# Even and odd tokens: v two tokens to a row, q and k as 96 rows, diagonal key blocks shared by two heads

## The chip, the core and the metric

The kernel runs on one core of a Trainium2 chip. The metric is the device time of one execution in microseconds. The engines are PE (TensorE matmuls; its weight loads are listed apart as PEld), ACT (ScalarE), DVE (VectorE), POOL (GpSimd, which here issues nearly all DMAs, and those that cast float32 to bf16 in flight) and SP (which issues most of the output DMAs).[...]

## What is computed

Attention with two kinds of heads over 4 batches, 8 heads, 768 tokens and head size 64, and then a soft mixture of experts over slots (8 experts of 4 slots). A "retrieval" head sees all earlier tokens; a "streaming" head sees the first 4 tokens and the last 64.

```
scores = q @ k.T / 8
keep   = causal                                   # retrieval heads
keep   = causal & (col < 4 | row - col < 64)      # streaming heads
a      = softmax(where(keep, scores, -1e9))
x      = concat over heads of a @ v               # 3072 x 512

logits = x @ phi                                  # 3072 x 32
slots  = softmax over tokens(logits).T @ x        # 32 x 512
y[e]   = relu(slots[e] @ w1[e]) @ w2[e]           # 512 -> 1024 -> 512
out    = softmax over slots(logits) @ y           # 3072 x 512
```

q, k and v are 6.3 MB each in float32, w1 and w2 16.8 MB each, and the output is 6.3 MB. Which heads are retrieval heads is data, read from a tensor, so every causal block is computed for every head, and the masks are made on the chip.

## The kernel before, in words

The unit of work is a pair of heads n of one batch (16 pairs). The two heads lie on partitions 0 to 63 and 64 to 127 of the transposed tiles, so a score matmul (L167, contraction over 64 rows) of one head uses one half of the array's rows. The order is written out by hand (L320 to L392): in step n the scores and exponentials of pair n are interleaved with the product with v of pair n-1.

Loading (L106 to L119). q and k come as 64 partitions for a head, 12 tokens (3 KB in float32) to a row. `load_v` (L116) brings four heads of v in one DMA, one token (256 bytes) to a partition and block: tile `vb` is [128, 4 heads, 6 blocks of 128 tokens, 64 + 2], the last two columns being ones. The weights come through `w_load` (L129), a few to a step: w1 of all experts, then w2 of experts 0 to 4, 12 more DMAs of 1 MB (as bf16) behind w1[0]. w2 of experts 5 to 7 is loaded in halves (L398) into the places of tiles that are done: of the masks (`msk`, free after the last mask) and of the two `pT` tiles (free after the product with v). All of these DMAs go through the one queue of POOL.

Transposing (L135 to L151). For each pair and each of q and k: 24 matmuls of 64x64 against the identity into a PSUM tile of tag `tr` (two buffers), then one copy to SBUF that puts the tokens in order: q by DVE (L148), k by ACT (L151).

Scores and exponentials (L160 to L172). The 21 causal blocks of 128 keys x 128 queries come in six chunks of up to 512 columns a head. Chunk c of both heads takes two PSUM banks (tag `sc`, two buffers), and one ACT instruction exponentiates it into `pT`. Chunks 0 to 2 hold the blocks on and next to the diagonal and are multiplied by 0/1 masks on DVE (L174 to L184). Streaming heads lose farther blocks through `vf` (L157), a copy of v that is zeroed for them by `fmask`.

Product with v (L186 to L194). For query block i and head hh, i+1 matmuls with 65 columns (64 of v and the column of ones, whose sum is the softmax denominator), 42 a pair. `norm` (L196) divides three blocks of both heads at a time.

Step n, on PE in this order: S0, product of blocks 0 to 2 of pair n-1 (and for n mod 4 = 2 the logits of the batch before), S1, transposes of q for pair n+1, S2, block 3, transposes of x of pair n-2, S3, transposes of k for n+1, S4, block 4, S5, block 5 (and for n mod 4 = 3 the dispatch of tokens to slots). ACT copies Tk of n+1 between E4 and E5; DVE takes norm, copy of Tq, masks, copy of x, masks, `vf`, norm. Setup (L253 to L305) builds the identity, the mask values and the masks of the first two heads; those of the others are made in steps 0 to 2, and small tables in step 3 (`setup_late`).

After the last pair (L428 on): last product with v, last logits, slot sums, first layer (w1), second layer (`second`, L508, experts 4 to 7: first the left half of the columns, then the right), and the output rows, left halves of the first 12 of 24 rows a partition first.

Of the kernel before, what the change touches and what calls it, by code (L numbers as in the profile page):

```python
# [19 lines left out]
NPT = 2688  # L20

CHUNKS = [
    (0, 512, [(0, 0, 2), (1, 1, 2)]),
    (512, 512, [(2, 2, 2), (3, 3, 2)]),
    (1024, 384, [(4, 4, 2), (5, 5, 1)]),
    (1408, 512, [(0, 2, 4)]),
    (1920, 512, [(1, 3, 3), (3, 5, 1)]),
    (2432, 256, [(2, 4, 2)]),
]
BLK = {}  # L30
for _o, _l, _parts in CHUNKS:
    for _j, _i0, _n in _parts:
        for _x in range(_n):
            BLK[_j, _i0 + _x] = _o
            _o += 128
# [3 lines left out]
def kernel(  # L39
# [39 lines left out]
    w2s = [single([P, 8, DM], BF16, f"w2_{e}") for e in range(NE - 3)] + [None] * 3  # L79
# [11 lines left out]
    msk = single([P, H, 640], BF16, "msk")  # L91
    fmask = single([P, H, 4, 66], BF16, "fmask")
# [7 lines left out]
    r0 = single([P, H], F32, "r0")  # L100
    thr = single([P, H], F32, "thr")
    vbs = [single([P, 4, 6, 66], BF16, f"vb{i}") for i in range(3)]
# [3 lines left out]
    def load_qk(pairs, order="qk"):  # L106
        b, h, c = pairs[0] // 4, 2 * (pairs[0] % 4), 2 * len(pairs)
        t = raw.tile([P, 2, 2, S], BF16, tag="raw", name="raw")
        for which in order:
            src, d, z = (q, qraw, 0) if which == "q" else (k, kraw, 1)  # L110
            nc.gpsimd.dma_start(t[:, z, :len(pairs)],  # L111
                                src[b, h:h + c].rearrange("(y h) (p s) d -> (h p) y (s d)", h=2, s=12))
            for x, n in enumerate(pairs):
                d[n] = t[:, z, x]

    def load_v(m):  # L116
        b, h = m // 2, 4 * (m % 2)
        nc.gpsimd.dma_start(vbs[m % 3].rearrange("p h j d -> p (h j) d")[:, :, :D],  # L118
                            v[b, h:h + 4].rearrange("h (j p) d -> p (h j) d", p=P))  # L119
# [8 lines left out]
    def w_load(upto):  # L128
        while wi[0] < min(upto, 2 * NE - 3):  # L129
            e = wi[0] % NE  # L130
            dst, src = ((w1s, w1v), (w2s, w2v))[wi[0] // NE]
            nc.gpsimd.dma_start(dst[e], src[e])
            wi[0] += 1

    def transposes(n, which):  # L135
        src = (qraw if which == "q" else kraw)[n]
        tp = trp.tile([P, 12, 64], BF16, tag="tr", name="tp" + which)
        for s in range(12):
            for hh in range(2):
                po = slice(64 * hh, 64 * hh + 64)  # L140
                nc.tensor.transpose(tp[po, s, :], src[po, 64 * s:64 * s + 64], ident[po, po])  # L141
        return tp

    def evac(n, which, tp):
        dst = qkT.tile([P, S], BF16, tag="T" + which, name="T" + which)
        o, i = dst.rearrange("c (p s) -> c p s", s=12), tp.rearrange("c s p -> c p s")
        if which == "q":
            nc.vector.tensor_copy(o, i)  # L148
            qT[n] = dst
        else:  # L150
            nc.scalar.copy(o, i)  # L151
            kT[n] = dst

    def vfar(n):
        h = 2 * (n % 4)
        t = vfp.tile([P, 2, 4, 66], BF16, tag="vf", name="vf")
        nc.vector.tensor_mul(t, vb(n)[:, :, :4, :], fmask[:, h:h + 2])  # L157
        vf[n] = t

    def scores(n, c):  # L160
        o, ln, parts = CHUNKS[c]
        sc = scp.tile([P, 2, 512], F32, tag="sc", name="sc")
        at = 0
        for j, i0, cnt in parts:
            for hh in range(2):
                po = 64 * hh
                nc.tensor.matmul(sc[:, hh, at:at + 128 * cnt], kT[n][po:po + 64, j * 128:(j + 1) * 128],  # L167
                                 qT[n][po:po + 64, i0 * 128:(i0 + cnt) * 128], start=True, stop=True)
            at += 128 * cnt
        if c == 0:  # L170
            pT[n] = ptp.tile([P, 2, NPT], BF16, tag="pT", name="pT")
        nc.scalar.activation(pT[n][:, :, o:o + ln], sc[:, :, :ln], ACT.Exp, scale=scale)  # L172

    def mask(n, c):  # L174
        h = 2 * (n % 4)
        if c == 0:
            x, m = pT[n][:, :, 0:512], msk[:, h:h + 2, 0:512]
        elif c == 1:
            x = pT[n][:, :, 512:1024].rearrange("p h (a c) -> p h a c", a=2)
            m0 = msk[:, h:h + 2, 256:512]  # L180
            m = bass.AP(tensor=m0.tensor, offset=m0.offset, ap=[m0.ap[0], m0.ap[1], [0, 2], [1, 256]])
        else:
            x, m = pT[n][:, :, 1024:1408], msk[:, h:h + 2, 256:640]
        nc.vector.tensor_mul(x, x, m)  # L184

    def pvmm(n, i):  # L186
        if i % 3 == 0:
            pv[n] = pvp.tile([P, 3, 2, 65], F32, tag="pv", name="pv")
        for hh in range(2):
            for j in range(i + 1):  # L190
                vv = vb(n) if i - j <= 1 else vf[n]
                o = BLK[j, i]
                nc.tensor.matmul(pv[n][:, i % 3, hh, :], pT[n][:, hh, o:o + 128], vv[:, hh, j, :D + 1],  # L193
                                 start=(j == 0), stop=(j == i))  # L194

    def norm(n, half):  # L196
        b, h = n // 4, 2 * (n % 4)
        if h == 0 and half == 0:
            xb[b] = xp.tile([P, 6, DM], BF16, tag="xb", name="xb")
        rs = small.tile([P, 3, 2, 1], F32, tag="rs", name="rs")  # L200
        nc.vector.reciprocal(rs, pv[n][:, :, :, 64:65])  # L201
        nc.vector.tensor_mul(  # L202
            xb[b][:, 3 * half:3 * half + 3, h * D:(h + 2) * D].rearrange("p i (h d) -> p i h d", h=2),
            pv[n][:, :, :, :64], rs.to_broadcast([P, 3, 2, 64]))
# [47 lines left out]
    diff = single([P, 256], F32, "diff")  # L252
    nc.gpsimd.iota(diff, pattern=[[1, 256]], base=0, channel_multiplier=-1,  # L253
# [15 lines left out]
    V.tensor_single_scalar(ident, diff[:, :P], 0.0, op=ALU.is_equal)  # L269
    one_row = single([1, P], BF16, "one_row")  # L270
    V.memset(one_row, 1.0)
    sk = single([P, 1], F32, "sk")
    sk2 = single([P, 1], F32, "sk2")
    ge = single([P, 256], BF16, "ge")
    grade = single([P, 640], BF16, "grade")
    V.tensor_single_scalar(rne, ri.rearrange("p (h c) -> p h c", c=2), 0.0, op=ALU.not_equal)
    V.tensor_tensor(rrow1, rne[:, :, 0], rne[:, :, 1], op=ALU.max)
    rb = trp.tile([P, H], F32, tag="tr", name="rb")
    nc.tensor.matmul(rb, one_row, rrow1, start=True, stop=True)
    V.tensor_single_scalar(ge, diff, 0.0, op=ALU.is_ge)  # L280
    V.scalar_tensor_tensor(grade[:, 256:512], diff, float(window), ge, op0=ALU.is_lt, op1=ALU.mult)
    V.tensor_add(grade[:, 256:512], grade[:, 256:512], ge)
    V.tensor_copy(grade[:, 512:640], grade[:, 256:384])
    V.tensor_single_scalar(sk, diff[:, 0:1], float(-n_sink), op=ALU.is_gt)
    V.tensor_scalar(sk2, sk, 2.0, None, op0=ALU.mult)
    V.scalar_tensor_tensor(grade[:, :256], ge, sk2, grade[:, 256:512], op0=ALU.mult, op1=ALU.max)
    V.tensor_copy(r1, rb)
    V.tensor_scalar(thr, r1, -1.0, 2.0, op0=ALU.mult, op1=ALU.add)
    V.tensor_scalar(r0, r1, sk, None, op0=ALU.max)

    def head_mask(h):
        V.tensor_scalar(msk[:, h], grade, thr[:, h:h + 1], None, op0=ALU.is_ge)

    for which in ("k", "q"):
        evac(0, which, transposes(0, which))
    for h in range(2):
        head_mask(h)
    def far_mask(n):
        h = 2 * n
        V.tensor_copy(fmask[:, h:h + 2, 1:], r1[:, h:h + 2].rearrange("p (h a d) -> p h a d", a=1, d=1).to_broadcast([P, 2, 3, 66]))  # L300
        V.tensor_copy(fmask[:, h:h + 2, 0], r0[:, h:h + 2].rearrange("p (h d) -> p h d", d=1).to_broadcast([P, 2, 66]))

    for t in vbs:
        V.memset(t[:, :, :, D:], 1.0)
# [15 lines left out]
    for n in range(NP):  # L320
# [16 lines left out]
        if n >= 1:  # L337
            for i in range(3):
                pvmm(last, i)
# [6 lines left out]
        if n >= 1:  # L346
            norm(last, 0)
# [3 lines left out]
        mask(n, 0)  # L351
# [4 lines left out]
        if n >= 1:  # L356
            pvmm(last, 3)
        if n >= 2:
            x_transpose(n - 2)
        mask(n, 1)  # L360

        scores(n, 3)
        if 0 < n < NP - 1:
            tk = transposes(n + 1, "k")
        mask(n, 2)

        scores(n, 4)
        if 0 < n < NP - 1:
            evac(n + 1, "k", tk)
        if n >= 1:  # L370
            pvmm(last, 4)
# [6 lines left out]
        if n >= 1:  # L378
            pvmm(last, 5)
# [4 lines left out]
        if n == 0:  # L384
            evac(1, "q", transposes(1, "q"))
            evac(1, "k", transposes(1, "k"))
        if n < 3:
            far_mask(n + 1)
            for h in (2 * n + 2, 2 * n + 3):
                head_mask(h)  # L390
# [10 lines left out]
    w2s[5] = single([P, 8, DM], BF16, "w2_5", tag="msk")  # L401
# [12 lines left out]
    def copies(y, t):  # L414
        g, b0 = y % 3, 2 * (y // 3)
        t = bank(t)
        for x in range(2):
            nc.tensor.matmul(t[:, 256 * x:256 * x + 256], sum4[32 * g:32 * g + 32],  # L418
                             expT[32 * g:32 * g + 32, b0 + x], start=True, stop=True)
# [9 lines left out]
    for i in range(3):  # L429
        pvmm(last, i)  # L430
# [3 lines left out]
    for i in range(3, 6):  # L434
        pvmm(last, i)
# [169 lines left out]
```

The softmax here doesn't subtract the row's maximum and nothing guards it: scores larger than these inputs give would overflow.

## Time and profile before

| | |
|---|---|
| median of 3 runs | 157.21 us (156.84 to 157.72) |
| the profiled execution | 157.49 us, its span 155.7 us |
| PE busy | 118.2 us (76%), 2239 matmuls |
| ACT busy | 109.8 us (71%), 148 instructions |
| DVE busy | 106.8 us (69%), 247 instructions |
| POOL busy | 41.1 us (26%), 57 instructions |
| DMA | 32.85 MB written, mean 211 GB/s; HBM read 52.49 MB |
| exponentials L172 | 96, 83.4 us on ACT |
| product with v L193 | 672 matmuls, 27.5 + 25.3 us on PE |
| copies of Tq L148 | 16, 956 ns each on DVE |
| v loads L118 | 8 of 384 KB, 13.0 us from issue to landing, 1451 ns of POOL each |

Busy times of one engine are sums over instructions. A busy PE is no PE at its peak, since matmuls are pipelined: in the timeline the distance between two starts tells more than a duration. The DMA rate counts bytes written; most loads read twice as many (float32 in, bf16 out). "A <- B" in the waits means that A stood idle until B was done, with total, number and longest wait. The chain of work that ended last is followed back from the last instruction; what stands in it set the end, in this one execution.

### The profile page before, as it was taken

How to read it: one execution, taken by the hardware profiler on the slowest of the kernel's cores; microseconds unless marked ns; L12 is line 12 of the kernel's file. 1: busy time of each engine (PE TensorE's matmuls, PEld its weight loads, DVE VectorE, ACT ScalarE, POOL GpSimd, SP SyncE). 2: the span in 40 equal slices, each digit the busy share in tenths (PEclk: the TensorE clock that was granted, in tenths of full speed). 3: DMA queues.
4: the chain of work that ended last, by engine and by line, in shares of the span. 5: the costliest groups of instructions: out<-in, count | busy, mean ns of one | idle time of the engine just before them, and what ended most of it. 6: DMA issues, size and time to landing. Idle time of an engine off the chain costs nothing. (4 is left out here: it accounts for less than half of the span.)

```text
span 155.7 us, 5051 instructions
## 1 busy us (share of the span) xinstructions
PE 118.2 (76%) x2239; PEld 74.6 (48%) x2239; DVE 106.8 (69%) x247; ACT 109.8 (71%) x148; POOL 41.1 (26%) x57
## 2 busy tenths in 40 slices
PE   6756598878697979977979979778987897449500
PEld 2324365555465645755656556555633476214300
DVE  2896269999987869978769979678735414429700
ACT  3286489979799998999898999999451512408700
POOL 7673043720350260170084200000480000700000
PEclk9975559999999999999999999999999999956975
DMA  3999999999999999999999999999999999977995
GB/s 54 155 184 203 172 218 203 196 187 189 212 219 202 188 216 198 186 222 195 186 219 200 185 211 223 213 217 215 210 223 190 199 196 199 240 290 283 404 355 183
DMA packets 40535, 32.85 MB, mean 211 GB/s; under 512 B 26050, under 2 KB 37826, under 8 KB 38594
## 3 DMA queue, kind: packets, MB, share of 16 engines
q0 software_dynamic: 38208, 27.82, 115.1%
q1 hardware_dynamic: 2306, 4.72, 8.1%
q8 instruction: 17, 0.28, 0.7%
q14 instruction: 4, 0.03, 0.1%
HBM read 52.49 MB, written 6.29 MB: 377 GB/s over the span
## 5 line engine op out<-in xcount | busy, mean ns | idle before, releaser
L172 ACT ACTIVATE pT<-sc 128x1024 bf16<-128x1024 f32 (+1 forms) x96 | 83.4, 923 | 9.3 <-PE sc L167 8.8
L167 PE MATMUL sc<-Tq,Tk 64*128 64x256 bf16 (+3 forms) x320 | 36.5, 292 | 13.6 <-ACT Tk L151 10.0
L193 PEld LDWEIGHTS <-pT 128*128 128x128 bf16 x672 | 24.9, 99 | 12.2 <-issue 8.0
L184 DVE TENSOR_TENSOR pT<-pT,msk 128x1024 bf16<-128x1024 bf16 (+1 forms) x48 | 29.3, 639 | 0.2 <-ACT pT L172 0.2
L193 PE MATMUL pv<-vb,pT 128*128 128x65 bf16 x352 | 27.5, 196 | 0.3 <-DVE xb L202 0.3
L193 PE MATMUL pv<-vf,pT 128*128 128x65 bf16 x320 | 25.3, 197 | 0.0
L167 PEld LDWEIGHTS <-Tk 64*128 64x128 bf16 x320 | 11.2, 95 | 22.6 <-ACT Tk L151 13.2
L141 PEld LDWEIGHTS <-raw 64*64 64x64 bf16 x768 | 15.9, 115 | 10.8 <-issue 7.4
L111 POOL DMA_DIRECT2D raw<-in_q_dram x10 | 6.4, 639 | 49.5 <-PE tpk L141 48.3
L148 DVE COPY Tq<-tpq 128x768 bf16<-128x768 bf16 x16 | 15.3, 956 | 4.8 <-PE tpq L141 4.6
L202 DVE TENSOR_TENSOR xb<-pv,rs 128x384 bf16<-128x384 f32 x32 | 17.8, 557 | 1.1
L151 ACT COPY Tk<-tpk 128x768 bf16<-128x768 bf16 x16 | 12.9, 805 | 5.0 <-PE tpk L141 5.0
L201 DVE RECIPROCAL rs<-pv 128x6 f32<-128x6 f32 x32 | 6.2, 193 | 11.9 <-PE pv L193 11.9
L118 POOL DMA_DIRECT2D vb<-in_v_dram x8 | 11.6, 1451 | 1.1 <-issue 0.9
L141 PE MATMUL tpk<-ident,raw 64*64 64x64 bf16 x384 | 9.8, 202 | 2.3 <-DVE Tq L148 1.3
L399 POOL DMA_DIRECT2D w<-in_moe_w_dram x6 | 5.2, 879 | 22.3 <-PE sc L167 20.1
L141 PE MATMUL tpq<-ident,raw 64*64 64x64 bf16 x384 | 9.6, 200 | 1.7 <-DMA raw<-in_q_dram 1.7
L541 PE MATMUL bank<-slot_out,expR 128*128 128x256 bf16 (+1 forms) x36 | 9.2, 368 | 1.9 <-DVE slot_out L556 0.5
L210 PE MATMUL tpx<-ident,xb 128*128 128x128 bf16 x96 | 8.1, 218 | 2.0 <-ACT expT L224 1.1
L211 DVE COPY xT<-tpx 128x768 bf16<-128x768 bf16 (+1 forms) x17 | 9.0, 528 | 0.8 <-PE tpx L210 0.8
L543 ACT ACTIVATE ot<-bank,rrow 128x512 f32<-128x512 f32 x6 | 3.9, 686 | 6.5 <-PE bank L541 6.5
L541 PEld LDWEIGHTS <-expR 128*128 128x128 bf16 x36 | 5.1, 153 | 6.3 <-issue 5.7
(86 smaller groups left out, 117.3 us busy)
## 6 DMA issues: line engine op xcount, KB each, us to landing
w<-in_moe_w_dram POOLq DMA_DIRECT2D x13, 1024.0 KB, 18.3
vb<-in_v_dram POOLq DMA_DIRECT2D x8, 384.0 KB, 13.0
w<-in_moe_w_dram POOLq DMA_DIRECT2D x6, 512.0 KB, 17.8
raw<-in_q_dram POOLq DMA_DIRECT2D x6, 384.0 KB, 10.2
raw<-in_k_dram POOLq DMA_DIRECT2D x6, 384.0 KB, 11.4
out_dram<-ot SPq DMA_DIRECT2D x2, 1024.0 KB, 4.6
out_dram<-oh SPq DMA_DIRECT2D x3, 512.0 KB, 6.3
out_dram<-oh POOLq DMA_DIRECT2D x2, 512.0 KB, 6.8
```

Source lines behind the costliest of these rows:

```text
L118: nc.gpsimd.dma_start(vbs[m % 3].rearrange("p h j d -> p (h j) d")[:, :, :D], v[b, h:h + 4].rearrange("h (j p) d -> p (h j) d", p=P))
L141: nc.tensor.transpose(tp[po, s, :], src[po, 64 * s:64 * s + 64], ident[po, po])
L148: nc.vector.tensor_copy(o, i)
L151: nc.scalar.copy(o, i)
L167: nc.tensor.matmul(sc[:, hh, at:at + 128 * cnt], kT[n][po:po + 64, j * 128:(j + 1) * 128], qT[n][po:po + 64, i0 * 128:(i0 + cnt) * 128], s ...
L172: nc.scalar.activation(pT[n][:, :, o:o + ln], sc[:, :, :ln], ACT.Exp, scale=scale)
L184: nc.vector.tensor_mul(x, x, m)
L193: nc.tensor.matmul(pv[n][:, i % 3, hh, :], pT[n][:, hh, o:o + 128], vv[:, hh, j, :D + 1], start=(j == 0), stop=(j == i))
L202: nc.vector.tensor_mul(xb[b][:, 3 * half:3 * half + 3, h * D:(h + 2) * D].rearrange("p i (h d) -> p i h d", h=2), pv[n][:, :, :, :64], rs. ...
L210: nc.tensor.transpose(tp[:, i * 128:(i + 1) * 128], xb[b][:, i, hp * 128:(hp + 1) * 128], ident)
L211: nc.vector.tensor_copy(xT[:, hp, i0 * 128:i1 * 128], tp[:, i0 * 128:i1 * 128])
L541: nc.tensor.matmul(op, er[r], slot_out[:, cs], start=True, stop=True)
```

## The change

Loads. v comes as two neighbouring tokens to a partition row, 512 bytes, in three blocks of 256 tokens; a v load is six DMAs, since for the second head of a pair the two halves of the partitions are swapped. q and k come as 96 partitions, 8 tokens (2 KB) to a row, the heads side by side.

Transposes. 16 a tensor and pair instead of 24, of 96 rows to 64 x 96. For q the copy to SBUF keeps the order (8 token residues, 6 blocks, 16 rows), so query columns within a block are permuted; score matmuls read them as runs of 16 elements. For k the copy by ACT separates even and odd tokens.

Scores. A key tile is 128 even or 128 odd tokens of a block of 256. For query block i = 2j only the first half of block j is causal; these halves of two heads are put on the two halves of the partitions of chunk 0: 12 matmuls 64 x 64 x 128. The other chunks: 4, 4, 8, 4 and 4 matmuls, 36 a pair instead of 20. ACT's elements stay 5376 a partition and pair. Chunks 0, 1 and 2 whole and half of chunk 3 are masked; in step 0 the masks come at the end of the step.

Product with v. 48 matmuls a pair instead of 42, and each head's six query blocks share one PSUM bank, which a matmul with zero weights and 396 columns clears first (two a pair). Even tokens take columns 0 to 64 of it (ones, then v), odd ones 1 to 65 (v, then ones), so that the denominator comes in two parts, which DVE adds. `norm` takes one head and all six blocks.

Setup and tail. Masks are built from distances in permuted order; they are larger (128 x 8192 + 128 x 3072 elements instead of 128 x 5120). `w2` of expert 4 has its place in the mask tile now, and is loaded after the last mask, ahead of the halves, no longer in the loop. The copies of the exponentials of the logits read `expT` in token order.

The built program has 128 matmuls more in the loop and the last pair; ACT's order is the same.

```diff
-    (0, 512, [(0, 0, 2), (1, 1, 2)]),
...
+    (0, 384, []),
+    (768, 512, [(0, 0, 1, 2), (0, 1, 1, 2)]),
+    (1792, 512, [(1, 0, 3, 2), (1, 1, 3, 2)]),
+    (2816, 512, [(0, 0, 5, 1), (0, 1, 5, 1), (2, 0, 5, 1), (2, 1, 5, 1)]),
+    (3840, 512, [(0, 0, 3, 2), (0, 1, 3, 2)]),
+    (4864, 256, [(1, 0, 5, 1), (1, 1, 5, 1)]),
...
-    w2s = [single([P, 8, DM], BF16, f"w2_{e}") for e in range(NE - 3)] + [None] * 3
+    w2s = [single([P, 8, DM], BF16, f"w2_{e}") for e in range(NE - 4)] + [None] * 4
...
-            nc.gpsimd.dma_start(t[:, z, :len(pairs)],
-                                src[b, h:h + c].rearrange("(y h) (p s) d -> (h p) y (s d)", h=2, s=12))
+            nc.gpsimd.dma_start(t[:96, z, :c], src[b, h:h + c].rearrange("h (p s) d -> p h (s d)", s=8))
...
-        nc.gpsimd.dma_start(vbs[m % 3].rearrange("p h j d -> p (h j) d")[:, :, :D],
-                            v[b, h:h + 4].rearrange("h (j p) d -> p (h j) d", p=P))
+        dst = vbs[m % 3][:, :, :, 1:129].rearrange("p (y x) j e -> p y x j e", x=2)
+        src = v[b, h:h + 4].rearrange("(y x) (j p t) d -> p y x j (t d)", x=2, j=3, t=2)
+        for y in range(2):
+            nc.gpsimd.dma_start(dst[:, y, 0], src[:, y, 0])
+            for a in range(2):
+                nc.gpsimd.dma_start(dst[64 * a:64 * a + 64, y, 1], src[64 - 64 * a:128 - 64 * a, y, 1])
...
+        for s in range(8):
             for hh in range(2):
-                nc.tensor.transpose(tp[po, s, :], src[po, 64 * s:64 * s + 64], ident[po, po])
+                nc.tensor.transpose(o, src[:, hh, s, :], ident[:96, :96])
...
-            nc.vector.tensor_copy(o, i)
+            nc.vector.tensor_copy(dst, tp.rearrange("c s p -> c (s p)"))
+            qT[n] = dst.rearrange("c (s i p) -> c i s p", s=8, i=6)
...
+            for x in range(6):
+                j, t = x // 2, x % 2
+                for hh in range(2):
+                    po = slice(64 * hh, 64 * hh + 64)
+                    nc.tensor.matmul(sc[po, x // 3, 128 * (x % 3):128 * (x % 3) + 128],
+                                     kT[n][po, j, t, 64 * hh:64 * hh + 64], qT[n][po, 2 * j], ...)
...
+            pv[n, hh] = pvp.tile([P, 6, 66], F32, tag="pv", name="pv")
+            nc.tensor.matmul(pv[n, hh].rearrange("p i d -> p (i d)"), zero[:, :P], zero[:, :396], start=True, stop=False)
+        for i in blocks:
+            for j in range(i // 2 + 1):
...
+                for t in range(2):
+                    nc.tensor.matmul(pv[n, hh][:, i, t:t + 65], pT[n][po, o:o + 128],
+                                     vv[po, hh, j, 65 * t:65 * t + 65], ...)
...
+        nc.vector.reduce_sum(rs, bass.AP(tensor=x.tensor, offset=x.offset, ap=[*x.ap[:2], [65, 2]]), axis=AX.X)
+        nc.vector.reciprocal(rs, rs)
+        nc.vector.tensor_mul(xb[b][:, :, h * D:(h + 1) * D], pv[n, hh][:, :, 1:65], rs.to_broadcast([P, 6, D]))
...
         scores(n, 0)
-            for i in range(3):
-                pvmm(last, i)
+            pvmm(last, 0, 0, 1, 2, 3)
         scores(n, 1)
-            norm(last, 0)
+            pvmm(last, 0, 4)
...
         scores(n, 2)
-            pvmm(last, 3)
+            pvmm(last, 0, 5)
+            norm(last, 0)
...
         scores(n, 3)
+        if n >= 1:
+            pvmm(last, 1, 0, 1, 2)
...
         scores(n, 4)
+            mask(n, 3)
...
-            pvmm(last, 4)
+            pvmm(last, 1, 3, 4)
         scores(n, 5)
-            pvmm(last, 5)
+            pvmm(last, 1, 5)
             norm(last, 1)
...
+    w2x = single([P, 2, 8, DM], BF16, "w2_45", tag="msk")
+    w2s[4], w2s[5] = w2x[:, 0], w2x[:, 1]
+    nc.gpsimd.dma_start(w2s[4], w2v[4])
     w_half(5, left)
...
-                             expT[32 * g:32 * g + 32, b0 + x], start=True, stop=True)
+                             expT[...].rearrange("e (i s p) -> e i p s", i=2, s=8), start=True, stop=True)
```

## The prediction

> **What bounds the kernel now.** I read the chain of work that ended last first, then the waits in total, then the timelines of PE and ACT for one pair of heads, then the stage table. S0 to S5 are the score matmuls of the six chunks of a pair (L167), E0 to E5 their exponentials (L172), Tq and Tk the transposed q and k, n the pair.
>
> The chain names what set the end:
>
> ```profile
> 113.05 2.59 POOL w L399 x3
> 115.64 22.18 DMA w<-in_moe_w_dram
> 137.82 0.04 issue
> 137.86 0.64 PE bank L513 x8
> ```
>
> The last half of w2 lands at 137.8 us, and the second product starts on it. But the bill of that wait is small:
>
> ```profile
> PE sc L167 <- ACT Tk L151: 10.0, 15, 0.9
> ACT pT L172 <- PE sc L167: 8.8, 17, 1.9
> DVE slot_out L560 <- PE bank L513: 4.5, 1, 4.5
> PE bank L513 <- DMA w<-in_moe_w_dram: 3.5, 2, 2.2
> ```
>
> PE waits 3.5 us for w2 in all. With w2 there in time, the rest of the tail would start 3.5 us sooner and no more: the work behind it hangs on when attention ends. So a second bound lies just behind the DMA, and it is the pace of the pairs. One undisturbed pair (n = 8), PE and then ACT:
>
> ```profile
> 61.90 0.39 PE L167 MATMUL sc<-Tq,Tk 64*128 64x256 bf16 x4 [0.23 <-ACT Tk L151]
> 62.70 0.39 PE L167 MATMUL sc<-Tq,Tk 64*128 64x256 bf16 x4
> 63.02 0.56 PE L141 MATMUL tpq<-ident,raw 64*64 64x64 bf16 x24
> 63.52 0.34 PE L167 MATMUL sc<-Tq,Tk 64*128 64x256 bf16 x4
> 64.48 0.39 PE L167 MATMUL sc<-Tq,Tk 64*128 64x512 bf16 x2
> 64.80 0.56 PE L141 MATMUL tpk<-ident,raw 64*64 64x64 bf16 x24
> 65.30 0.39 PE L167 MATMUL sc<-Tq,Tk 64*128 64x384 bf16 x4
> 67.61 0.39 PE L167 MATMUL sc<-Tq,Tk 64*128 64x256 bf16 x4 [0.80 <-ACT Tk L151]
> ```
>
> ```profile
> 61.72 5.14 ACT L172 ACTIVATE pT<-sc 128x512 bf16<-128x512 f32 x6
> 66.74 0.82 ACT L151 COPY Tk<-tpk 128x768 bf16<-128x768 bf16 x1
> ```
>
> ACT has no gap: six exponentials and the copy of Tk take 5.7 us, and that is this pair's period. But a loop through PE is nearly as long. S0 of the next pair needs Tk; ACT copies it after E4; E4 needs S4; and PE, in order, reaches the end of S4 only 3.79 us after S0 started (61.90 to 65.69). Then come about 0.1 to the start of E4, 0.92 for E4, 0.81 for the copy and 0.06 to S0: 1.89. The loop is 3.79 + 1.89 = 5.68. **Whatever PE does before S4 is no longer free.** A pair with logits (n mod 4 = 2) takes 6.78, the one after it 6.28, the other two 5.7: 24.46 for four (61.90 to 86.36).
>
> The DMA, one microsecond a row (busy columns, granted clock, DMA share, GB/s written):
>
> ```profile
> 53.00:54.00 1.00, 1.00 (x38) 0.75 (x32) 1.00 (x3) 1.00 (x2) 0.31 (x1) 1.00 2.04 183
> 54.00:55.00 1.00, 0.82 (x18) 0.53 (x14) 0.71 (x3) 1.00 (x2) 1.00 (x2) 1.00 2.33 181
> 56.00:57.00 1.00, 1.00 (x34) 0.74 (x34) 0.44 (x2) 0.96 (x2) 1.00 (x2) 1.00 1.36 212
> ```
>
> While a v load moves, the rate falls from about 213 to about 182 GB/s.
>
> [...] six N = 128 transposes (L210) take 0.50 us, less 0.22 for a single one: 56 ns each; eight pv matmuls (N = 65) start 33 ns apart.[...] the 12 logits matmuls (N = 256, three column groups) take 0.55 us from start to start[...].
>
> **The change, part by part.**
>
> *v in 512-byte rows.* Around 53 us the dip is (30 + 30 + 32 + 5) KB short of 213 GB/s in four microseconds, 0.46 us; around 31 to 40 two loads lose 1.15. That is 0.4 to 0.6 for each of 8 loads, 3 to 5 us in all; half of it[...] is 2 us (bounds 0 and 5). Each load is six DMAs instead of one; at 0.55 to 0.6 of POOL each (the w row has 0.56) that is 3.5 us instead of 1.45, on an engine that is busy 26%. q and k are queued behind v at the start; that costs the next q up to 1 us and is paid by v's faster landing: nothing.
>
> *w2[4] moved behind attention.* By 109.07 the queue has moved 109.07 x 195 = 21.3 MB of the 23.1 issued; 1.8 MB, 9 us, are waiting. w2[4] is 1.05 MB of that, 5 us, and goes behind the last mask; 2 more come off from v. So the queue still has about 2 us of work when the late loads (now 4.2 MB, 21 us at 200 GB/s) are issued. Their end is about T + 23, T being the last mask (109); the products want the last half at T + 24.5 (133.5 now, without waits). **The w2 wait goes: −3.5 us** (bounds −1 and −4). Next in line is the pace of attention.
>
> *PE before S4.* From starts in the timeline, before and then after: S0 0.33 → 0.42 (four N = 256 become six quadrant pairs at N = 128: 0.32 + 0.1 start-up); pv 0.47 → 0.64 (still 12, and a zeroing matmul of 396 columns, 0.165); S1 0.32; new here, six pv for block 4: 0.22; Tq 0.50 → 0.42 (16 of 96 columns[...], two column groups; 0.33 if perfectly paired, 0.66 if not at all); S2 0.27; pv 0.26 → 0.22; x transposes 0.43; S3 0.32 → 0.34 (eight N = 128); new before S4: zeroing and eight pv, 0.43; Tk 0.50 → 0.42; S4 0.39. **3.79 → 4.52.** With the 1.89 of ACT the loop is 6.41; ACT's own work stays at 5.7 (5376 elements before and after), so the loop now sets the pace: +0.7 in the two plain pairs. The logits pair adds 0.55 of PE and 0.35 for the tile that logits_exp frees, to 7.3 (+0.5); the next one 0.2, to 6.6 (+0.3). Four pairs: +2.25. From S0 of n = 6 (48.86) to n = 14 that is +4.5; n = 14 +0.5; n = 2 to 5, today held at 25.0 by DVE's mask building, +1.3. **Attention: +6.3.**
>
> *DVE.* Copy of Tq: 956 → about 551 (the xT row, same shape, contiguous): −0.4. Masks: 0.6 + 0.6 + 0.55 → 0.55 + 0.6 + 0.6 + 0.35: +0.4. A sum from PSUM per head: +0.4. That makes about 5.5 us a pair: hidden under 6.4, and not if PE were faster. Building masks: about 2 us more before the first mask and 0.8 more a pair until n = 3; ACT runs through E0 to E5 of pair 0 meanwhile, as those masks are put last. pv of pair 0 then waits until about 17 us, PE's S1 and E1 of pair 1 behind it, where today PE waits for q until 18.3 anyway. −0.4 (bounds −1 and +2).
>
> *The tail.* Six pv and two zeroing matmuls more in the last pair, and copies that read expT with a stride: +0.7 (bounds 0 and +2).
>
> **Sum.** 157.49 (the profiled execution: span 155.7 and 1.8 around it) − 3.5 + 6.3 − 0.4 + 0.7 = 160.6. The median of the runs shown is 157.21, 0.3 lower: I take 160.5.
>
> **Rivals.** *Faster: the loop stays hidden.* If transposes pair perfectly (0.33 twice), S0 costs nothing extra and pv is back at 0.40, the PE part is 4.1 and the loop 6.0; attention +1.5, and −3.5 of DMA shows through: 153.5 to 156.4. For it: the chain is DMA; PE is 76% busy. Against it: it needs every low end at once; the two zeroing matmuls alone are 0.33. The turning point is a gain of 3.5 over 13 pairs, a loop of some 6.15.
> *Same:* between these, 156.4 to 158.
> *Much slower: PE is worse than counted.* Unpaired transposes (0.66 twice) make the loop 6.9; and the query tiles are now read as runs of 16 elements, 192 bytes apart. Strided weight loads take 153 ns here (L541) against 97 plain; the same factor of 1.6 on the 1.2 us of score streaming up to S4[...] would add 0.7. Attention +11 to +17: 163.5 to 172. No trace shows such a moving read.
> *The rows do nothing:* v's dip stays. Then T + 24 against T + 24.5 is still no wait while attention is later: within 0.5 us of the forecast.
>
> **Numbers.** Forecast (158 to 163.5) 0.52; much slower 0.18; faster 0.18; same 0.12. A measurement tells 0.5%, 0.8 us, from no change. Range 155.3 to 167.5 leaves out about a tenth on each side; the forecast's own is 158 to 163.5.
>
> **What would show it.** A period of 6.3 to 6.5 between S0 of plain pairs, with ACT idle 0.6 to 0.8 before E4 for S4; S4 ending 4.5 after S0; no wait of the second product for w2; a shallower dip at v loads; a DMA gap before the last mask. I am wrong if plain pairs stay at 5.7 to 6.0, or if DVE or a v load stops PE.

## The result, and the profile after

193.22 us median (192.35 to 203.03, 4 runs) against 157.35 of the kernel before: slower by the factor 1.226 (95% interval 1.220 to 1.233). The forecast was 160.5, its range 155.3 to 167.5: the direction was right, the size was missed by 33 us. In some executions of the kernels below PE's clock stays low for longer than in others (its mean was 0.78 in that of 203.03 us, 0.85 in that of 192.35); the ratios leave these out, and where no ratio stands, the range of all executions is given or the profiled one is named.

The profiled execution of the changed kernel has a span of 190.6 us (before 155.7). From its page, the row of the granted clock, one digit for 4.8 us, and the shares of the chain that ended last:

```profile
PEclk9955555859999999999999999999997557978975
...
PE 17%; DVE 7%; issue 1%; ACT 0%
```

No DMA is left in that chain, where 22 us of w2 stood before. Its waits, in total, times and longest:

```profile
ACT pT L186 <- PE sc L183: 26.8, 42, 1.5
...
PE sc L177 <- ACT Tk L159: 10.7, 14, 0.9
...
DVE slot_out L629 <- PE bank L582: 1.1, 1, 1.1
```

The second product waits for w2 no more (the last slot_out waited 4.5 us before, now 1.1), and ACT waits three times as long for PE as before (8.8). A pair at full clock, n = 11 (0.2 us of transposes for the dispatch left out), on PE up to S4 and then on ACT:

```profile
100.44 0.52 PE L177 MATMUL sc<-Tq,Tk 64*64 64x128 bf16 x12 [0.88 <-ACT Tk L159]
100.89 0.34 PE L205 MATMUL pv<-zero 128*128 128x396 bf16 x1
101.16 0.63 PE L213 MATMUL pv<-vb,pT 64*128 64x65 bf16 x8
101.72 0.23 PE L213 MATMUL pv<-vf,pT 128*128 128x65 bf16 x2
...
101.95 0.39 PE L183 MATMUL sc<-Tq,Tk 64*128 64x256 bf16 x4
102.28 0.23 PE L213 MATMUL pv<-vf,pT 128*128 128x65 bf16 x2
102.35 0.39 PE L213 MATMUL pv<-vb,pT 128*128 128x65 bf16 x4
102.67 0.53 PE L150 MATMUL tpq<-ident,raw 96*64 96x96 bf16 x16
...
104.28 0.40 PE L183 MATMUL sc<-Tq,Tk 64*128 64x128 bf16 x8
104.61 0.34 PE L205 MATMUL pv<-zero 128*128 128x396 bf16 x1
104.89 0.63 PE L213 MATMUL pv<-vb,pT 64*128 64x65 bf16 x8
105.45 0.53 PE L150 MATMUL tpk<-ident,raw 96*64 96x96 bf16 x16
105.91 0.39 PE L183 MATMUL sc<-Tq,Tk 64*128 64x256 bf16 x4
```

```profile
102.39 1.02 ACT L186 ACTIVATE pT<-sc 128x1024 bf16<-128x1024 f32 x1 [0.53 <-PE sc L183]
...
106.34 1.02 ACT L186 ACTIVATE pT<-sc 128x1024 bf16<-128x1024 f32 x1 [0.60 <-PE sc L183]
```

ACT now waits for PE in several places of the pair, 0.60 us of it for S4. The form of the tile, rows x columns of the array, matters here, as e1, e5 and e12 measure: 64*64 and 64*128 are tiles of 64 rows, 128*128 one of 128; the group "x8" at 101.16 is named after its first product and holds four of 64 rows and four of 128. S0 to the end of S4 takes 5.67 us without those transposes (forecast 4.52), and the period of plain pairs is 7.48 (S0 at 46.39, 53.88 and 61.36) instead of 5.7.

Where the 34.9 us of span come from, by the starts of S0 in both traces:

| stretch | before | after | more |
|---|---|---|---|
| start to S0 of pair 1 | 14.75 | 16.21 | 1.5 |
| pairs 1 to 4 | 28.40 | 37.67 | 9.3 |
| pairs 5 to 14 | 61.38 | 77.44 | 16.1 |
| S0 of pair 15 to the product with the last slot_out | 34.47 | 41.90 | 7.4 |
| the rest, mostly output rows | 16.73 | 17.33 | 0.6 |

In pairs 1 to 4 another thing than the loop is at work. Four microseconds a row, PE alone (busy, clock, DMA share, GB/s), the changed kernel:

```profile
28.00:32.00 4.00, 4.00 (x52) 0.50 1.03 199
...
36.00:40.00 4.00, 3.65 (x43) 0.55 1.37 172
40.00:44.00 4.00, 4.00 (x61) 0.59 1.60 192
44.00:48.00 4.00, 3.12 (x65) 1.00 1.02 196
```

In the rows of half clock shown PE is busy for 91 to 100%. The kernel before is at 1.00 from 24 us on, with less of PE busy (3.66, 3.31, 2.97 and 2.85 of the 4 us from 24, 28, 36 and 40 us).

Three things are thus to be explained: a loop that is 1.1 us longer than forecast (7.48 for 6.41), half clock, and the tail.

### The profile page after: what moved, and what is told of

The parts are those of the page before. It is cut to its first block, busy times and chain, and to the rows that moved or that the text cites. A ratio compares the mean times of both kernels' runs of the same rounds, so it can differ in the third digit from the quotient of the medians.

```text
span 190.6 us, 5455 instructions
## 1 busy us (share of the span) xinstructions
PE 157.4 (83%) x2365; PEld 95.4 (50%) x2367; DVE 117.1 (61%) x330; ACT 113.7 (60%) x148; POOL 62.9 (33%) x97
## 5 line engine op out<-in xcount | busy, mean ns | idle before, releaser
L213 PEld LDWEIGHTS <-pT 128*128 128x128 bf16 (+1 forms) x768 | 35.8, 100 | 26.0 <-issue 17.3
L213 PE MATMUL pv<-vb,pT 128*128 128x65 bf16 (+1 forms) x512 | 47.2, 201 | 0.0
L183 PE MATMUL sc<-Tq,Tk 64*128 64x256 bf16 (+1 forms) x384 | 33.6, 267 | 1.5 <-ACT pT L186 1.5
L156 DVE COPY Tq<-tpq 128x768 bf16<-128x768 bf16 x16 | 8.9, 556 | 29.9 <-PE tpq L150 29.9
L126 POOL DMA_DIRECT2D vb<-in_v_dram x32 | 20.5, 643 | 3.1 <-DMA w<-in_moe_w_dram 3.1
L177 PE MATMUL sc<-Tq,Tk 64*64 64x128 bf16 x192 | 9.3, 236 | 13.2 <-ACT Tk L159 10.7
L150 PEld LDWEIGHTS <-raw 96*64 96x64 bf16 x512 | 14.3, 120 | 3.3 <-DMA raw<-in_k_dram 0.8
L177 PEld LDWEIGHTS <-Tk 64*64 64x64 bf16 x192 | 6.7, 116 | 15.8 <-ACT Tk L159 14.3
L124 POOL DMA_DIRECT2D vb<-in_v_dram x16 | 12.7, 796 | 4.7 <-DVE vb L365 4.1
L205 PE MATMUL pv<-zero 128*128 128x396 bf16 x32 | 11.9, 372 | 1.1 <-DVE xb L225 1.1
L150 PE MATMUL tpq<-ident,raw 96*64 96x96 bf16 x256 | 9.8, 227 | 0.4 <-DMA raw<-in_q_dram 0.4
```

The source lines that it names most:

```text
L124: nc.gpsimd.dma_start(dst[:, y, 0], src[:, y, 0])
L126: nc.gpsimd.dma_start(dst[64 * a:64 * a + 64, y, 1], src[64 - 64 * a:128 - 64 * a, y, 1])
L150: nc.tensor.transpose(o, src[:, hh, s, :], ident[:96, :96])
L177: nc.tensor.matmul(sc[po, x // 3, 128 * (x % 3):128 * (x % 3) + 128], kT[n][po, j, t, 64 * hh:64 * hh + 64], qT[n][po, 2 * j], start=True, ...
L183: nc.tensor.matmul(sc[:, hh, at:at + 128 * cnt], kT[n][po, j, t], qT[n][po, i0:i0 + cnt], start=True, stop=True)
L205: nc.tensor.matmul(pv[n, hh].rearrange("p i d -> p (i d)"), zero[:, :P], zero[:, :396], start=True, stop=False)
```

## The experiments

Each ran beside the kernel before on the same chip, whose medians were 157.1 to 158.0 us. A change of form below is a step, in PE's order, from a matmul of one tile form to one of another. Ahead of S4 the kernel before has 8 of them in a plain pair, the changed kernel 18: four of the ten more are in the zeroing and the products ahead of S1, two around block 4, four in the second head's zeroing and products. First the loop.

**e1, the own blocks' products over all rows.** In a query block's product with its own half block of keys:

```diff
-                po = slice(64 * hh, 64 * hh + 64) if own else slice(0, P)
+                po = slice(0, P)
```

> The diagonal blocks' products with v take all 128 rows in place of one head's 64 (so each of them also adds the other head's half: part of the computation is changed, the instruction count is not). Theory: the loop S0 to S4, E4, copy of Tk, S0 sets the pace, and what lengthens it beyond the forecast is the change between 64-row and 128-row matmuls within the product with v, about 0.2 us for each of the five diagonal pairs ahead of S4. Then S0 to the end of S4 falls from 5.67 to about 4.65 us, the plain period from 7.48 to about 6.5, and the time from 193 to about 178. Rival: the number of matmuls and weight loads sets PE's pace, and their rows don't matter: period 7.4 to 7.5, time 192 to 194.

177.13 us, ratio 1.114 (1.105 to 1.123); plain period 6.65 (S0 at 74.84 and 81.49). PE at the start of the next pair:

```profile
81.49 0.52 PE L177 MATMUL sc<-Tq,Tk 64*64 64x128 bf16 x12 [0.88 <-ACT Tk L159]
81.94 0.34 PE L205 MATMUL pv<-zero 128*128 128x396 bf16 x1
82.12 0.42 PE L213 MATMUL pv<-vb,pT 128*128 128x65 bf16 x8
82.38 0.23 PE L213 MATMUL pv<-vf,pT 128*128 128x65 bf16 x2
```

The same eight products start 0.26 us before the next group, where it was 0.56, and the zeroing takes 0.18 where it was 0.27. Number and columns are unchanged, the rows are more: so it isn't their amount that costs. In the plain pair S4 ends 4.84 us after S0 instead of 5.67: 0.83 us for eight changes of form less. (The products read the other head's keys too here.)

**e2, the second head's first products behind S4.** No work is taken out or added; zeroing and eight products move from before S4 to behind it:

```diff
         scores(n, 3)
-        if n >= 1:
-            pvmm(last, 1, 0, 1, 2)
...
-            pvmm(last, 1, 3, 4)
+            pvmm(last, 1, 0, 1, 2, 3, 4)
```

> The zeroing matmul and the first eight products of the second head are moved from between S3 and the transposes of k to behind S4; no work is added or removed. Theory (the loop through S4): 0.84 us leave the part ahead of S4 and lie in the time in which PE waits for E4 and the copy of Tk, so the plain period falls from 7.48 to about 6.7 and the time from 193 to about 181. Rival (PE's throughput is the bound, whatever the order): period and time stay, 192 to 194.

182.49 us, ratio 1.156 (1.150 to 1.163), plain period 6.77 (S0 at 35.10, 41.87, 48.66). With the same work on every engine, and as many changes of form in a pair, the pair is 0.7 us shorter: the loop through S4 sets the pace, not PE's amount of work.

**e5, the six own products of a head together.** They and a 64-row zeroing matmul come right behind S0 (and S3), which have 64 rows themselves; the loop over blocks then has only 128-row products:

```diff
+        for i in (0, 2, 4):
+            for t in range(2):
+                nc.tensor.matmul(pv[n, hh][:, i, t:t + 65], pT[n][po, 128 * (i + t):...], vb(n)[po, hh, ...], ...)
...
-            for j in range(i // 2 + 1):
+            for j in range((i + 1) // 2):
```

> The six 64-row products of a head's diagonal blocks are put together, with a zeroing matmul of 64 rows ahead of them, right behind score matmuls (which are 64-row too); the 128-row products follow. Nothing is left out. Theory: it is the change between 64-row and 128-row matmuls that costs some 0.1 us each way, not the 64-row matmul; five of six changes into and out of 64 rows vanish, S0 to the end of S4 falls from 5.67 to about 4.8, the plain period from 7.48 to about 6.7, the time to about 180. Rival: a 64-row product costs 0.1 us in itself; then period and time stay within 0.2 us a pair of the changed kernel, 190 to 193.

Ratio 1.143 (1.134 to 1.152); plain period 6.82 (S0 at 41.99 and 48.82). The four executions took 180.0, 181.2, 192.2 and 197.3 us, with mean granted clocks of 0.87, 0.85, 0.77 and 0.74. PE in a plain pair of the first:

```profile
41.99 0.52 PE L177 MATMUL sc<-Tq,Tk 64*64 64x128 bf16 x12 [0.94 <-ACT Tk L159]
42.44 0.34 PE L205 MATMUL pv<-zero 64*128 64x396 bf16 x1
42.62 0.35 PE L209 MATMUL pv<-vb,pT 64*128 64x65 bf16 x6
42.90 0.30 PE L220 MATMUL pv<-vb,pT 128*128 128x65 bf16 x4
...
45.24 0.40 PE L183 MATMUL sc<-Tq,Tk 64*128 64x128 bf16 x8
45.47 0.33 PE L205 MATMUL pv<-zero 64*128 64x396 bf16 x1
```

Six 64-row products in a row take 0.28 with the one change behind them: they are not dear by themselves. What costs is going from one form to another and back: S3 takes 0.23 us with a zeroing of its own form behind it (45.24 to 45.47), where the changed kernel's takes 0.33 with one of 128 rows (104.28 to 104.61). S0, in tiles of 64*64, still takes 0.45 with 64*128 behind it. S4 ends 5.02 us after S0, 0.65 less for seven changes of form less.

**e9, 64-row own products in the kernel before.** The converse, in the kernel that has none (this leaves out half of the keys of the diagonal blocks):

```diff
-                nc.tensor.matmul(pv[n][:, i % 3, hh, :], pT[n][:, hh, o:o + 128], vv[:, hh, j, :D + 1], ...)
+                po = slice(0, 64) if i == j else slice(0, P)
+                nc.tensor.matmul(pv[n][:, i % 3, hh, :], pT[n][po, hh, o:o + 128], vv[po, hh, j, :D + 1], ...)
```

> The kernel before with one thing of the change: the products of a block with its own keys use 64 rows of the array instead of 128 (this leaves out the upper half of the keys of those blocks). No instruction is added, none streams more columns. Theory (a change between 64-row and 128-row products costs PE about 0.1 us each way): ahead of S4 such products stand in seven places, so about 1.4 us more, the loop goes from 5.7 to about 7.1 us, 13 pairs give +18, the wait for w2 (3.5) disappears under it: 170 to 174 us. Rival (the change's loss is in its layout, the zeroing and the 128 further matmuls, not in 64-row products): the same number of matmuls with the same columns takes the same time, 157.5 us.

203 to 215 us, far more than forecast. The reason is the clock. PE, PEld, DVE, ACT, POOL, clock, DMA share and GB/s in two stretches of 40 us:

```profile
60.00:100.00 40.00, 40.00 (x484) 23.75 (x483) 20.97 (x42) 24.40 (x31) 6.74 (x8) 0.50 0.82 113
100.00:140.00 40.00, 40.00 (x484) 23.64 (x481) 20.75 (x42) 24.52 (x30) 6.03 (x9) 0.50 0.93 163
```

PE has no gap for 80 us and runs at half clock throughout, 9.45 us a plain pair; the mean granted clock is 0.57 to 0.65 in all four executions (0.89 and more in the kernel before beside them). The rival (nothing happens) is out, but the price at full clock can't be read from this.

**e12, the same with a dense run of matmuls ahead of pair 3.**

```diff
+        if n == 3:
+            keep_busy(pvp.tile([P, 512], F32, tag="pv", name="idle"), 12)
         scores(n, 0)
```

> The kernel before with 64-row own products as in e9 (the upper half of the keys of those blocks is left out), and twelve zero matmuls of 512 columns in a row ahead of S0 of pair 3[...]. e9 stood at half clock for all of attention although PE had no gap, so what 64-row products cost at full clock is not to be read there. Theory A (PE without gaps is not enough for the clock to rise, a dense run of full-width matmuls is): the clock goes to full in or behind the burst at 33 to 39 us and stays there, plain pairs take about 7.1 us (5.7 before, seven places at 0.2), and the total is about 178. Theory B (the changes between 64 and 128 rows themselves pull the clock down again): half clock soon returns, pairs of 9.45 us as in e9, total about 210 to 215.

```profile
33.93 3.91 PE L266 MATMUL idle<-zero 128*128 128x512 bf16 x12
37.77 0.39 PE L167 MATMUL sc<-Tq,Tk 64*128 64x256 bf16 x4
38.00 0.76 PE L194 MATMUL pv<-vb,pT 64*128 64x65 bf16 x6
...
39.17 0.41 PE L167 MATMUL sc<-Tq,Tk 64*128 64x256 bf16 x4
39.51 0.56 PE L141 MATMUL tpq<-ident,raw 64*64 64x64 bf16 x24
...
40.28 0.24 PE L194 MATMUL pv<-vf,pT 128*128 128x65 bf16 x2
...
40.94 0.51 PE L211 MATMUL tpx<-ident,xb 128*128 128x128 bf16 x6
...
44.50 0.39 PE L167 MATMUL sc<-Tq,Tk 64*128 64x256 bf16 x4 [0.28 <-ACT Tk L151]
```

The same places in the kernel before (S0 at 61.90, S1 at 62.70):

```profile
62.23 0.36 PE L193 MATMUL pv<-vb,pT 128*128 128x65 bf16 x6
...
63.79 0.24 PE L193 MATMUL pv<-vf,pT 128*128 128x65 bf16 x2
...
64.05 0.50 PE L210 MATMUL tpx<-ident,xb 128*128 128x128 bf16 x6
```

The clock rose in the burst (0.50 from 34 to 36 us, 0.93 from 36 to 38, 1.00 from 38 to 46), and this one pair shows the price: 6.73 us (37.77 to 44.50), where the kernel before has 5.7. The twelve products of blocks 0 to 2 take 1.17 us from the first to S1, where they take 0.47 in the kernel before; the form changes eight times on that way, not once: 0.70 for seven changes. S0 ahead of them takes 0.23 instead of 0.33, as no change follows it. Block 3 (40.28 to 40.94) takes 0.66 and not 0.26, with four changes and not none. **A change between 64*128 and 128*128 costs 0.10 us**, all three times. It isn't the number of rows alone: S1, four matmuls like those of S0, takes 0.34 with the 64*64 transposes behind it (39.17 to 39.51), which have 64 rows too. The forecast of 7.1 took 14 changes more ahead of S4; there are ten, and 1.03 us. Then came what theory B forecast: some 10 us after it had risen the clock fell to half again (0.63 from 46 to 48 us, 0.50 from 48 to 100), though PE had waited only 0.28 us in all that time. But from about 122 to 132 us it was full once more (the mean from 100 to 140 is 0.63), with no burst ahead, so neither theory is shown to be the cause. The total was 201.9 to 212 us.

**e11, only the zeroing, in the kernel before.**

```diff
             pv[n] = pvp.tile([P, 3, 2, 65], F32, tag="pv", name="pv")
+            nc.tensor.matmul(pv[n].rearrange("p i h d -> p (i h d)"), zero[:, :P], zero[:, :390], start=True, stop=True)
```

> The kernel before with a zeroing matmul of 390 columns ahead of each half of the product with v: two a pair, both ahead of S4, nothing else changed. It asks whether PE work ahead of S4 shows one for one in the period of the pairs of the kernel before, as the prediction held. Theory: 0.33 us more[...] to 0.56 (0.28 each, as the changed kernel shows it), period of plain pairs 6.0 to 6.25 instead of 5.7, attention +4 to +7, of which 3.5 lie under the wait for w2: 158.5 to 161. Rival (ACT sets the pace and has some slack): period 5.7 to 5.8, 157.5.

159.61 us, ratio 1.013 (1.007 to 1.019).

```profile
69.39 0.39 PE L167 MATMUL sc<-Tq,Tk 64*128 64x256 bf16 x4 [0.79 <-ACT Tk L151]
69.71 0.34 PE L189 MATMUL pv<-zero 128*128 128x390 bf16 x1
69.89 0.35 PE L194 MATMUL pv<-vb,pT 128*128 128x65 bf16 x6
...
73.11 0.39 PE L167 MATMUL sc<-Tq,Tk 64*128 64x384 bf16 x4
...
75.41 0.39 PE L167 MATMUL sc<-Tq,Tk 64*128 64x256 bf16 x4 [0.79 <-ACT Tk L151]
```

Each takes 0.18 us among 128-row products. S4 ends 4.11 us after S0 instead of 3.79, and the period goes from 5.70 to 6.02: 0.32 us ahead of S4 is 0.32 us of period. The method of the forecast, and its estimate of 0.165 for this matmul, hold. PE waits 0.66 to 0.80 us for Tk in most pairs here, and the clock stays full from 23 us to the tail (mean of the whole execution 0.92).

Next, the copies of the exponentials behind attention. In the changed kernel a pair of these matmuls takes 1.0 us (before 0.32).

**e10, the strided read alone, in the kernel before.**

```diff
-                             expT[32 * g:32 * g + 32, b0 + x], ...
+                             expT[32 * g:32 * g + 32, b0 + x].rearrange("e (i s p) -> e i p s", i=2, s=8), ...
```

> The kernel before with only the strided read of the logits' exponentials in the six copies behind attention (the copies come out in another order of tokens; nothing is left out). Theory: a pair of these matmuls takes 1.0 us on PE instead of 0.32, 4.1 us in all; before the second layer 3.5 us of waiting for w2 lie under it, so that wait vanishes and the time rises by about 0.5 to 1.5 us: 158 to 159. Rival (PE's slow copies in the changed kernel are its half clock, not the stride): 0.32 us a pair as before, the w2 wait as before, 157.5.

160.73 to 164.55 us in five executions, where the kernel before took 156.81 to 158.35. The groups by form of the one of 160.73, with total and mean ns:

```profile
L418 PE MATMUL bank<-expT,sum 32*128 32x256 bf16 x12 | 5.4, 624 | 0.0
L481 PE MATMUL bank<-w,siT 128*32 128x512 bf16 x64 | 5.2, 498 | 0.0
```

In the kernel before these are 273 and 380 ns. Each copy takes 1.0 us, three at full clock and three at half: it is the stride, and the changed kernel's 624 ns are the same. The last two of the six run side by side (1.0 us for both, 0.32 in the kernel before), so the six cost 3.4 us more, not 4.1. The forecast of 158 to 159 was too low, since the clock is at half from about 117 to 127 us (0.50 from 118 to 126; 1.00 there in the kernel before), behind the first slow copies and over the first layer too (L481, 5.2 us, not 3.6). The w2 wait is gone, as the theory expected.

**e3, read in order, written with a stride.** ACT and DVE put the tokens in order instead:

```diff
-                             expT[...].rearrange("e (i s p) -> e i p s", i=2, s=8), ...
+                             expT[...], ...
+        o = o.rearrange("c b (i p s) -> c b i s p", i=2, s=8)
```

> In the tail the copies of the logits' exponentials read expT in its own order again, and ACT or DVE puts the tokens in order while writing. Theory: the read with a stride of 32 bytes makes each pair of copy matmuls take 1.01 us in place of 0.32; six of them are 4 us of the tail, and a PE that crawls is the reason for a second spell at half clock (147 to 159 us), worth another 2. So 187 to 189 us, copies at 0.3 us again. Rival: the tail is longer because of the half clock alone, which has another cause; then the copies stay near 0.5 us and the time is 192 to 193. Third: ACT's strided write costs as much as PE's strided read: ACT's copies go from 0.59 to over 1 us and the time stays.

192.69 us in the profiled execution (all four: 192.69 to 201.10), as without the edit (192.35). PE's copies are back at 336 ns, but now ACT's are slow:

```profile
L497 ACT CAST expR<-bank 128x512 bf16<-128x512 f32 x5 | 11.9, 2578 | 5.1 <-PE bank L489 5.1
```

586 ns is their mean in the changed kernel. Writing single bf16 elements 16 bytes apart takes ACT 2.0 us more a copy, and the tail gains nothing: the third outcome of the three.

**e6, written in runs of 16.** Read in order, kept in the permuted order in runs of 16 elements; the output rows pick their tokens with a stride of 3:

```diff
+        o = expR.rearrange("c (s b i p) -> c b i s p", s=8, b=B, i=6)[:, b0:b0 + 2, 2 * g:2 * g + 2]
...
-        e = expR.rearrange("c (p r) -> c r p", r=24)[:, r]
+        e = expR.rearrange("c (s p k) -> c k s p", s=8, k=3)[:, r // 8, r % 8]
```

> The copies of the logits' exponentials read expT in order and are written in runs of 16 elements into an expR ordered by token residue, from which the output rows are read with a stride of 3 in place of 24. Nothing is left out. Theory: the strided read on PE is 4 us of the tail (1.01 us a pair of copy matmuls in place of 0.32), and runs of 16 cost ACT little (0.6 to 0.7 us a copy, where single elements cost 2.4): 187 to 189 us. Rival: runs of 16 cost ACT as much as single elements, 190 us and more.

```profile
L496 ACT CAST expR<-bank 128x512 bf16<-128x512 f32 x5 | 2.9, 585 | 9.1 <-PE bank L489 9.1
```

In its stage the theory held: copies of 0.32 us on PE, 585 ns on ACT, and 36.7 us from S0 of pair 15 to the last slot_out's product, where the changed kernel has 41.9. In total it missed: 196.81 us (1.245; 1.239 to 1.252), since the clock stayed at half until about 66 us (0.50 from 26 to 62, 0.53 from 62 to 66), in pairs of 10.8 us. The edit touches nothing there, so the spell of half clock in the first pairs is not set by the loop alone.

**e4, a filled gap.** PE idles 2.15 us ahead of S0 of pair 1; five zero matmuls are put there.

> Five matmuls on zeros are put where PE waits 2.15 us ahead of S0 of pair 1, nothing else. Theory: gaps in PE's work let its clock fall to half from 10 us on and stay there until 32 and again from 36 to 43 us; without that gap the clock is full by about 20 us, pairs 1 to 3 take 7.5 to 8 us in place of 10, and the time is 186 to 188. Rival: the clock is low because of what PE executes (matmuls that wait on weights and changes of rows), not because of gaps: full clock still only after 32 us, time 192 to 194.

The clock was full by pair 2 (1.00 from 28 to 34 us, pairs of 7.5 us at 24.05 and 31.54), but then came two waits of 0.9 us, 3 us apart (for Tk ahead of 31.54, for q ahead of 34.74). From 35 to 72 us the clock was half (0.50 from 36 to 70), with PE 97% busy from 36 to 70. This is the execution of 200.36 us; the shortest of the four took 192.43, no less than the changed kernel. The theory's first half held, its gain did not.

**e7, all mends together.** e5's grouping, e6's copies, e2's late second head, and the transposes of x behind S5:

> Grouped diagonal products, copies in runs, all of the second head's product behind S4, and the transposes of x behind S5. Nothing is left out. Theory (the loop through S4): S0 to the end of S4 is about 3.9 us, the loop 5.8, next to ACT's own 5.7; attention then takes as long as in the kernel before but for its start (1.5 us and a spell of half clock), the tail about 1.4 more, and the wait for w2 is gone: 157 to 162 us. Rival (PE's throughput or DVE is the next bound): plain periods of 6.3 and more, 165 and more.

167.69 us, ratio 1.051 (1.040 to 1.062): about 26 us better than the change as it stands, and still slower than before. Three pairs of it, with logits (n = 10), with the dispatch (11) and plain (4), in the same columns as for e9:

```profile
78.83:85.94 7.11, 6.40 (x137) 4.71 (x138) 5.26 (x14) 6.11 (x10) 3.55 (x6) 1.00 1.41 206
85.94:92.47 6.53, 6.50 (x132) 4.61 (x133) 5.00 (x15) 5.90 (x8) 3.03 (x6) 1.00 1.12 199
39.10:45.43 6.33, 5.86 (x124) 4.39 (x124) 5.97 (x25) 5.88 (x8) 4.08 (x8) 1.00 1.40 186
```

The forecast of 157 to 162, 5.8 us a plain pair, took the loop alone, and missed. In the plain pair ACT and PE are each busy for 5.9 of 6.33 us (DVE too in this one, 5.0 in n = 9), and ACT still waits 0.28 us for S1 there (n = 9). In the pair with the dispatch PE is busy for 6.50 of 6.53, and the one behind it takes 7.12, PE waiting 0.72 for DVE's norm. With the loop shortened there is no single next bound: ACT's own work is near in plain pairs, PE's amount of work in those with the dispatch.

**e8, v in 512-byte rows in the kernel before.** One DMA of 1536 rows for a load, the rest of the kernel as it was (the products take other tokens of v, in the same number and shape):

```diff
-                            v[b, h:h + 4].rearrange("h (j p) d -> p (h j) d", p=P))
+                            v[b, h:h + 4].rearrange("h (j p t) d -> p (h j) (t d)", p=P, t=2))
```

> The kernel before with v loaded in 512-byte rows, one DMA of 1536 descriptors a load in place of 3072; products then take the wrong tokens of v (part of the computation is changed, counts and shapes of all instructions are not). Theory: v's rows give 2 us of DMA time (bounds 0 and 5), the last half of w2 lands that much earlier, and up to 3.5 of it is seen: 154 to 156 us, and the rate during v loads no longer dips to 180 GB/s but to about 200. Rival: destination runs of 256 bytes are as slow as those of 128, the rate dips as before, and the time stays 157.

155.22 us, ratio 0.984 (0.977 to 0.992). PE's wait for w2 falls from 3.5 to 0.9 us, and the time with it. So the wider rows by themselves gain about 2.5 us. Around the load at 53 us the rate falls to 194 GB/s and not to 181; around those at 31 to 37 us single microseconds are still at 181 and 185 (173 and 179 in the kernel before). A version that has them and reads the right tokens was not tried: with even and odd tokens in tiles of their own, a diagonal block is half empty, and unless halves are shared as in the change, ACT has them to exponentiate in full.

## Why the prediction was wrong, point by point

In the profiled execution 192.35 us stand against the sum of 160.6. By the stretches of the sum the 31.7 us of miss are: start 1.9, attention 19.0 (half clock about 7.7 of it, by the estimate below, the loop the rest), tail 10.8.

- *What bounds the kernel, the loop, −3.5 for w2:* right. PE time ahead of S4 shows one for one in the period (e11, and by moving in e2); the loop is PE up to the end of S4 plus 1.89 (5.67 + 1.89 = 7.56, measured 7.48). The w2 wait went, DMA stood nearly still from 132 to 137 us ahead of the last mask (2 GB/s from 132 to 136), as foreseen, and e8 has the 2 us of v at 2.5 (that half of the dip would go was an estimate that no trace of before showed). The last half of w2 landed about 24.5 us behind the last mask (forecast 23; 29 before). The products wanted it only 34 us behind it, as the tail had grown by itself, so the narrow margin of the forecast, 23 against 24.5, was not put to the test.
- *"PE before S4 ... 3.79 → 4.52":* **this step failed**, in its terms for the product with v. They took the distance of 128-row products in a row (33 ns) for each of them. Zeroing and product measured 1.07, 0.40, 0.20 and 0.84 for 0.64, 0.22, 0.22 and 0.43. The diagonal products have 64 rows, and stand among 128-row ones: ten more changes of form ahead of S4 than in the kernel before, at 0.10 us (e12; e1 takes out eight of them and 0.83 us, e5 seven and 0.65). 4.52 + 1.0 + 0.08 of transposes (0.46 for 0.42) + 0.03 of S0 is 5.63, measured 5.67. The sum had no term for a change of form but one, which I called start-up: the 0.1 of S0's 0.42.
- *Attention +6.3:* from S0 of pair 6 to that of pair 15, at full clock, 14.3 (I had 5.0), by the same term: 1.0 us a pair too little in nine pairs.
- *Not in the sum at all: half clock.* By estimate it made about 7.7 of the 37.7 us of pairs 1 to 4 (37.7 less four periods of 7.5). Its cause stays open. Waits alone don't explain it: e11 waits 0.7 to 0.8 us in most pairs at full clock. e9 and the kernel before differ in one edit, and e9 stays at half (mean clock 0.57 to 0.65, there 0.89 and more): there the 64-row products or their changes of form (14 more in a pair) bring it about; which of the two, no run tells. In the changed kernel it is less clear. With ten changes more in a pair it holds the full clock from 43 us on; e2, with as many, does so from 32 us; e5, with fewer, from 31 us in one execution, but has mean clocks of 0.77 and 0.74 in two others (the changed kernel 0.78 to 0.86). That PE is busy is not enough: in e12 the clock is up within the 3.9 us of the burst, in e9 it stays at 0.50 through 80 us without a gap. What makes it rise or fall stays open; so does why e6 stayed at half longer than the kernel it comes from (to about 66 us, not 43).
- *Tail +0.7 (bounds 0 and +2), beside −3.5:* **this term failed too.** It measured +7.4 up to the last slot_out, −3.5 for the wait among it, so about +11: 2.9 until the first copy (pair 15 and the first of the last products); 5.5 from there to the first layer (3.4 for the six copies, as in e10, 0.6 for the second head's last products, most of the rest half clock); 2.6 in the first layer and behind it (the first layer 5.9 instead of 3.6 us: half clock). The strided read was named and put far too low. The half clock there isn't its doing alone: e3 and e6, whose copies read in order, have such a spell in the tail too (146 to 159 us, 154 to 165 us). Strides were priced for queries, where runs of 16 elements cost nothing (S1 0.32 from 94.32 to 94.64 us, as in the kernel before); here single elements 32 bytes apart are read, in 1.0 us instead of 0.32 (e10). What makes the difference was not shown.
- *"Much slower" rival:* its two mechanisms, unpaired transposes and slow query reads, did not happen (0.46 us for 16 transposes, 0.32 for S1). The time passed its upper end by another way.
- *Start −0.4:* +1.5, inside its bounds (PE waits 2.15 us for Tq behind the masks). *DVE hidden:* right; copies of Tq took 556 ns, 551 forecast.

## What to carry to other kernels

When a matmul is split by rows to save work on another engine, count how often the tile form changes in PE's order, and price each change (0.10 us here), not only the columns that stream; put matmuls of one form together. Read access patterns by the step of the innermost element: here runs of 16 elements were free (S1 0.32 us as before), single elements 32 bytes apart took 1.0 us where reading in order took 0.32. And a period at full clock is no forecast for stretches where the clock may fall (pairs of 10.8 us at half clock in e6, 7.48 at full in the changed kernel): check the granted clock of each stage before adding up.

## What the runs showed of the hardware

- A change between matmuls of tile form 64*128 and 128*128: 0.10 us at full clock (e12); from 64*128 to 64*64 about as much (S1 0.34 with it, S0 0.23 without, e12).
- A moving operand of bf16 read at steps of 32 bytes: 1.0 us for two matmuls of 256 columns at full and at half clock alike, 0.32 in order (e10).
- ACT writing bf16 from PSUM at steps of 16 bytes: 2.58 us for 512 elements a partition; in runs of 16 elements 0.585 (e3, e6).
- PE at half clock (0.50) without a gap for 80 us (e9), full clock with a gap of 0.79 us in a pair of 6.02 us (e11).
